# Softmax without its maximum, and layer normalisation moved behind the output product, in a RWKV5 plus SoLU kernel

## The chip, the cores and the metric

The kernel runs on one core of a Trainium2 chip. The metric is device time in microseconds of one execution; lower is better. A "median" below is over the executions of one kernel in one set of runs. 2% is the margin below which two kernels count as the same. On one core all runs of a set share a chip and the runs of the kernel before.

In the profile's lines PE is TensorE, PEld its weight load, DVE is VectorE, ACT is ScalarE, POOL is GpSimd. L806 is a line of that kernel's source, so the same operation has other numbers in other kernels. A "round" is one value of the loop's index `i`.

## The reference

An RWKV5 attention (batch 4, 8 heads, 768 tokens, head size 48) feeds a SoLU feed-forward block with 3072 tokens, 384 model columns and 1024 inner columns:

```python
# attention, per token t:  y = r (state + u k v^T);  state = w * state + k v^T
# ... x = y as (3072, 384)
h = x @ w_in                                   # (3072, 1024)
h_max = np.max(h, axis=-1, keepdims=True)
e = np.exp(h - h_max)
sm = e / (np.sum(e, axis=-1, keepdims=True) + 1e-09)
solu = h * sm
mu = np.mean(solu, axis=-1, keepdims=True)
var = np.mean((solu - mu) ** 2, axis=-1, keepdims=True)
ln = (solu - mu) / np.sqrt(var + 1e-06) * g_ln
return (ln @ w_out).astype(np.float32)
```

## The kernel before

Work comes in 24 units of 128 tokens. The loop is a software pipeline: in round `i` it prepares unit `i+2`, makes the scores of unit `i+1`, the attention output of unit `i`, the inner product `h_ps` and the softmax of unit `j = i-2`, and the output product of unit `l = i-5`. The weights arrive as 64-bit words and are converted on the chip in rounds -2 to 5 (`convert_a` to `convert_d`, on three engines); `g_ln` is multiplied into `w_out`. A flag `bad` chooses at the very end whether a slow general path must run; with these inputs it never does.

```python
    def diagonal(i):                     # ScalarE: eight diagonals of the scores
        ...
        for h in range(H):
            nc.scalar.activation(out=AT[:, h, :], in_=ident, func=ACT.Copy, scale=X["own"][:, h])

    def ffn_in(i):
        h_ps = psH.tile([128, dff], F32, name="h_ps")      # one buffer
        # ... 6 matmuls into h_ps
        nc.vector.tensor_reduce(out=nmax, in_=h_ps, axis=AX.X, op=ALU.max, negate=True)
        nc.scalar.activation(out=e, in_=h_ps, func=ACT.Exp, bias=nmax, accum_out=se)

    def unit(i):
        nc.vector.tensor_scalar_add(rs, se, 1e-9)
        nc.vector.reciprocal(out=rs, in_=rs)
        nc.vector.scalar_tensor_tensor(out=solu, in0=h_ps, scalar=rs, in1=e, ..., accum_out=tot)
        nc.vector.tensor_scalar_mul(nmu, tot, -1.0 / dff)
        nc.scalar.activation(out=sq, in_=solu, func=ACT.Square, bias=nmu, accum_out=ss)
        # ... GpSimd: var, then rstd = var ** -0.5

    def normalise(i):
        nc.vector.tensor_scalar(out=X["solu"], in0=X["solu"], scalar1=nmu, scalar2=rstd,
                                op0=ALU.add, op1=ALU.mult)

    def turn_ln(i):      # 8 transposes into t_ps (TensorE), copied to lnT (VectorE, ScalarE)
    def ffn_out(i):      # 8 matmuls of lnT with w_out into o_ps, copied out, stored

    for i in range(-2, N + LA + LO):
        # ... turn_r, sum_own, turn_k of unit i+2; convert_d; convert_a, convert_b
        diagonal(i + 2)
        # ... decay_k, convert_c, weigh
        turn_ln(l); ffn_in(j); scores(i + 1); unit(j)
        if drain and l + 1 < N:
            turn_ln(l + 1)
        ffn_out(l); normalise(j); finish(i)
```

(`finish` makes the attention output y, its copy xT on ScalarE, and the state.)

Of the kernel before, what the change touches and what calls it, by code (L numbers as in the profile page):

```python
# [9 lines left out]
F32 = mybir.dt.float32  # L10
U32 = mybir.dt.uint32
ACT = mybir.ActivationFunctionType
ALU = mybir.AluOpType
AX = mybir.AxisListType
# [4 lines left out]
def general_path(  # L19
# [191 lines left out]
    def prepare(i):  # L211
        b, c = units[i]
        kt, rt, vt = kpads[i % NLD], rpads[i % NLD], vts[i % NLD]
        X = live[i] = {}
        kT = apool.tile([128, HP, T], F32, name="kT")
        rT = apool.tile([128, HP, T], F32, name="rT")
        for src, dst in ((kt, kT), (rt, rT)):
# [3 lines left out]
            nc.scalar.copy(out=dst, in_=ps)  # L221
        X["kT"], X["rT"] = kT, rT
        X["z"] = {}
        for ls in LEVELS:
# [172 lines left out]
def direct_path(  # L397
# [16 lines left out]



    nc = tc.nc
    B, H, S, D = r.shape
    T = 128
# [3 lines left out]
    dm = H * D  # L423
    dff = moe_w_in.shape[1]
    KD = dm // 128
    KF = dff // 128
    NX = 512
    LA, LO = 2, 3
    LOW, HIGH = 0.75, 1.25

    FLOOR, CEIL = 2.0 ** -15, 122880.0

    const = ctx.enter_context(tc.tile_pool(name="const", bufs=1))
    apool = ctx.enter_context(tc.tile_pool(name="apool", bufs=2))
    fpool = ctx.enter_context(tc.tile_pool(name="fpool", bufs=2))
    wpool = ctx.enter_context(tc.tile_pool(name="wpool", bufs=2))
    small = ctx.enter_context(tc.tile_pool(name="small", bufs=4))
    psA = ctx.enter_context(tc.tile_pool(name="psA", bufs=2, space=PSUM))
    psH = ctx.enter_context(tc.tile_pool(name="psH", bufs=1, space=PSUM))
    psM = ctx.enter_context(tc.tile_pool(name="psM", bufs=4, space=PSUM))  # L440
# [6 lines left out]
    units = [(b, c) for c in range(C) for b in range(B)]  # L447
# [6 lines left out]
    def load(i, which="krv"):  # L454
        b, c = units[i]
        for t, src, n in ((kpads, k, "k"), (rpads, r, "r"), (vts, v, "v")):
            if n in which:
# [8 lines left out]
    w_out_sb = const.tile([128, KF, dm], F32, name="w_out_sb")  # L466
# [5 lines left out]
                        in_=u.rearrange("h d -> (h d)").partition_broadcast(128))  # L472
# [4 lines left out]
    def words(x):  # L477
# [5 lines left out]
    pieces = [(w_in_sb[:, c, ts(n, NX)], w_in_w[ts(c, 128), ts(n, 2 * NX)], None)  # L483
              for n in range(dff // NX) for c in range(KD)]
# [79 lines left out]
    def double(x):  # L564
        for j in range(7):
# [7 lines left out]
                            op0=ALU.max, op1=ALU.min)  # L573
# [27 lines left out]
    def make_wt():  # L601

        nc.gpsimd.memset(wt, 0.0)
        for q in range(2):
            rows = slice(q * P, q * P + D)
            nc.gpsimd.tensor_copy(out=wt[rows, :, q, :],
                                  in_=pw[rows, 0, 7].unsqueeze(2).to_broadcast([D, HP, D]))

    bad = flag.tile([1, 1], mybir.dt.int32, name="bad")

    def check_range():
        nc.sync.dma_start(out=wrow, in_=w.rearrange("h d -> (h d)").partition_broadcast(1))

        ok = small.tile([1, dm], F32, tag="ok", name="ok", bufs=1)
        ok2 = small.tile([1, dm], F32, tag="ok2", name="ok2", bufs=1)
        nc.vector.tensor_single_scalar(out=ok, in_=wrow, scalar=LOW, op=ALU.is_ge)
        nc.vector.tensor_single_scalar(out=ok2, in_=wrow, scalar=HIGH, op=ALU.is_le)
        nc.vector.tensor_mul(ok, ok, ok2)
        all_ok = small.tile([1, 1], F32, tag="all_ok", name="all_ok", bufs=1)
        nc.vector.tensor_reduce(out=all_ok, in_=ok, axis=AX.X, op=ALU.min)  # L620
        nc.vector.tensor_scalar(out=bad, in0=all_ok, scalar1=-1.0, scalar2=1.0,
                                op0=ALU.mult, op1=ALU.add)

    live = {}

# [20 lines left out]
    def diagonal(i):  # L646
        X = live[i]
        AT = X["AT"] = apool.tile([128, H, T], F32, name="AT", bufs=3)
        for h in range(H):
            nc.scalar.activation(out=AT[:, h, :], in_=ident, func=ACT.Copy, scale=X["own"][:, h])  # L650
# [8 lines left out]
    def turn_k(i):  # L659
        X = live[i]  # L660
        X["kT"] = apool.tile([128, HP, T], F32, name="kT")
        ps = psM.tile([128, HP, T], F32, tag="m", name="tk_ps")
        for a in range(HP):
            nc.tensor.transpose(ps[:, a, :], pair(X["kp"], a), ident)  # L664
        nc.scalar.copy(out=X["kT"], in_=ps)  # L665
# [62 lines left out]
    def ffn_in(i):  # L728
        X = live[i]
        h_ps = psH.tile([128, dff], F32, name="h_ps")  # L730
        for n in range(dff // NX):
            for j in range(KD):
                nc.tensor.matmul(h_ps[:, ts(n, NX)], X["xT"][:, j, :], w_in_sb[:, j, ts(n, NX)],  # L733
                                 start=(j == 0), stop=(j == KD - 1))
        st = small.tile([128, 8], F32, name="st")
        nmax, se, rs, tot, nmu, ss, var, rstd = X["st"] = [st[:, n : n + 1] for n in range(8)]
        nc.vector.tensor_reduce(out=nmax, in_=h_ps, axis=AX.X, op=ALU.max, negate=True)  # L737
        e = fpool.tile([128, dff], F32, name="e")
        nc.scalar.activation(out=e, in_=h_ps, func=ACT.Exp, bias=nmax, accum_out=se)  # L739
        X["h"], X["e"] = h_ps, e  # L740

    def unit(i):
        X = live[i]
        nmax, se, rs, tot, nmu, ss, var, rstd = X["st"]
        h_ps, e = X["h"], X["e"]
        nc.vector.tensor_scalar_add(rs, se, 1e-9)
        nc.vector.reciprocal(out=rs, in_=rs)
        solu = X["solu"] = fpool.tile([128, dff], F32, name="solu", bufs=LO + 2)
        nc.vector.scalar_tensor_tensor(out=solu, in0=h_ps, scalar=rs, in1=e,  # L749
                                       op0=ALU.mult, op1=ALU.mult, accum_out=tot)  # L750
        nc.vector.tensor_scalar_mul(nmu, tot, -1.0 / dff)  # L751
        sq = fpool.tile([128, dff], F32, name="sq", bufs=1)
        nc.scalar.activation(out=sq, in_=solu, func=ACT.Square, bias=nmu, accum_out=ss)  # L753
        nc.gpsimd.tensor_scalar(out=var, in0=ss, scalar1=1.0 / dff, scalar2=1e-6,  # L754
                                op0=ALU.mult, op1=ALU.add)
        nc.gpsimd.tensor_tensor(out=rstd, in0=var, in1=neg_half, op=ALU.pow)  # L756

    def normalise(i):
        X = live[i]
        nmax, se, rs, tot, nmu, ss, var, rstd = X["st"]  # L760
        nc.vector.tensor_scalar(out=X["solu"], in0=X["solu"], scalar1=nmu, scalar2=rstd,  # L761
                                op0=ALU.add, op1=ALU.mult)


    def turn_ln(i):
        X = live[i]
        lnT = X["lnT"] = fpool.tile([128, KF, 128], F32, name="lnT")
        for g in range(KF // 4):
            t_ps = psM.tile([128, 4, 128], F32, tag="m", name="t_ps")
            for f in range(4):  # L770
                nc.tensor.transpose(t_ps[:, f, :], X["solu"][:, ts(4 * g + f, 128)], ident)  # L771
            if g % 2 == 0:
                nc.vector.tensor_copy(out=lnT[:, ts(g, 4), :], in_=t_ps)
            else:
                nc.scalar.copy(out=lnT[:, ts(g, 4), :], in_=t_ps)

    def ffn_out(i):
        b, c = units[i]
        X = live.pop(i)
        o_ps = psM.tile([128, dm], F32, tag="m", name="o_ps")  # L780
        for f in range(KF):
            nc.tensor.matmul(o_ps, X["lnT"][:, f, :], w_out_sb[:, f, :],  # L782
                             start=(f == 0), stop=(f == KF - 1))
        o = fpool.tile([128, dm], F32, name="o")
        nc.scalar.copy(out=o, in_=o_ps)
        nc.sync.dma_start(out=out[ds(b * S + c * T, T), :], in_=o)


    N = len(units)
    ahead = 5  # L790
    todo = list(range(len(pieces)))
    conversions = {-2: 1, -1: 1, 0: 2, 1: 2, 2: 3, 3: 3, 4: 2}
    now = []
    decay_k(0)
    for i in range(-2, N + LA + LO):
        j, l = i - LA, i - LA - LO
        drain = i >= N + LA - 1
        if i == 0:
            nc.sync.dma_start(out=g_sb, in_=moe_g_ln.rearrange("(c p) -> p c", p=128))
        if 0 <= i and i + 4 < N:  # L800
            load(i + 4)
        if i + 2 < N:
            turn_r(i + 2)
            if i == -2:
                weigh(0, nc.vector)
            sum_own(i + 2)  # L806
            turn_k(i + 2)
        for p in now:
            convert_d(p)
        now = [todo.pop(0) for _ in range(conversions.get(i, 0))]  # L810
        for p in now:
            convert_a(p)
            convert_b(p)
            if ahead < len(pieces):
                load_weights(ahead)
                ahead += 1
        if i + 2 < N:
            diagonal(i + 2)
        if i + 3 < N:
            decay_k(i + 3)  # L820
        for p in now:
            convert_c(p)
        if i + 3 < N:
            weigh(i + 3, nc.gpsimd)
        if i == -1:
            make_wt()
        if i == 10:
            check_range()
        if 0 <= l and not i > N + LA - 1:
            turn_ln(l)  # L830
        if 0 <= j < N:
            ffn_in(j)
        if 0 <= i + 1 < N:
            scores(i + 1)
        if 0 <= j < N:
            unit(j)
        if drain and l + 1 < N:
            turn_ln(l + 1)
        if 0 <= l:
            ffn_out(l)  # L840
        if 0 <= j < N:
            normalise(j)
        if 0 <= i < N:
            finish(i)
    return bad


# [40 lines left out]
```

## Time and profile before

| | before |
|---|---|
| median of 3 runs | 429.55 us (428.15 to 429.98) |
| span of the profiled execution | 427.9 us, mean granted clock 0.964 |
| busy share: TensorE, VectorE, ScalarE, GpSimd | 93, 50, 43, 30% |
| one steady round | 16.07 us, all TensorE |
| fifth h_ps begins (end of the start) | 101.47 us |
| TensorE ends | 422.90 us |

The table is to be read as three stages. In the start (a quarter of the span) weights are still being converted and TensorE waits for other engines. In the steady rounds TensorE is the whole chain. In the end no input is left and TensorE drains. A change counts only where it shifts the last wait of its stage. The profile's lines are shown in the prediction.

### The profile page before, as it was taken

The numbers are of one execution on the slowest core, as the hardware profiler recorded it, in microseconds if no ns is written. First come the engines' busy times: TensorE is split into PE (matmuls) and PEld (weight loads), VectorE is DVE, ScalarE is ACT, GpSimd is POOL, SyncE is SP. The second block draws the span as 40 slices with busy tenths as digits, with TensorE's granted clock in tenths as the row PEclk, the third lists the DMA queues.
The fourth block names the chain that finished last, engine by engine and source line by source line (L and its number), as shares of the span: only waits on it lengthen the run. The fifth ranks groups of instructions, "written<-read, shape, count | busy, mean of one in ns | idle before, by whom it ended". The sixth has DMA issues, their size and how long they took to land.

```text
span 427.9 us, 7198 instructions
## 1 busy us (share of the span) xinstructions
PE 395.9 (93%) x2853; PEld 249.7 (58%) x2853; DVE 212.4 (50%) x391; ACT 185.0 (43%) x422; POOL 128.7 (30%) x167
## 2 busy tenths in 40 slices
PE   2579397799999999999999999999999999999995
PEld 1466353556756756756756756756756756565562
DVE  6787987743643645642642642642642633343410
ACT  1775377544344344344344344344344442233310
POOL 4587544524124124124124134134134000000000
PEclk9868778899999999999999999999999999999999
DMA  8999891003303303303213213123120000000011
GB/s 170 270 199 222 182 103 20 0 2 74 65 12 74 64 12 74 63 13 74 62 15 74 60 16 76 47 29 75 34 41 20 20 1 20 20 18 11 8 40 43
DMA packets 81592, 25.92 MB, mean 61 GB/s; under 512 B 76557, under 2 KB 79758, under 8 KB 81550
## 3 DMA queue, kind: packets, MB, share of 16 engines
q1 hardware_dynamic: 81406, 25.18, 29.3%
q8 instruction: 24, 0.39, 0.4%
q10 hardware_dynamic: 144, 0.20, 0.1%
q14 instruction: 18, 0.15, 0.1%
HBM read 20.65 MB, written 4.72 MB: 59 GB/s over the span
## 4 chain that ended last, share of the span: by engine, by line
PE 80%; DVE 13%; POOL 2%; issue 2%; ACT 1%; DMA 1%; POOLq 0%; ACTq 0%; DVEq 0%
PE o_ps L782 30%; PE h_ps L733 26%; PE y_ps L703 7%; PE t_ps L771 5%; PE at L675 5%; PE kv_ps L719 4%; DVE ma L516 3%; DVE ma L518 2%; PE tr_ps L656 2%; PE tk_ps L664 2%; DVE mag L512 1%; DVE tab L567 1%; POOL rku L639 1%; POOL rku L640 1%; DVE solu L749 1%
## 5 line engine op out<-in xcount | busy, mean ns | idle before, releaser
L733 PE MATMUL h_ps<-w_in_sb,xT 128*128 128x512 f32 x288 | 133.4, 615 | 9.0 <-DVE solu L749 9.0
L782 PE MATMUL o_ps<-w_out_sb,lnT 128*128 128x384 f32 x384 | 129.5, 491 | 0.0
L782 PEld LDWEIGHTS o_ps<-w_out_sb,lnT 128*128 128x128 f32 x384 | 71.2, 190 | 47.9 <-issue 1.0
L733 PEld LDWEIGHTS h_ps<-w_in_sb,xT 128*128 128x128 f32 x288 | 55.0, 198 | 70.4 <-issue 70.4
L737 DVE TENSOR_REDUCE st<-h_ps 128x1 f32<-128x1024 f32 x24 | 29.4, 1223 | 92.6 <-PE h_ps L733 92.6
L739 ACT ACTIVATE e<-h_ps,st 128x1024 f32<-128x1024 f32 x24 | 26.8, 1115 | 94.8 <-DVE st L737 94.8
L650 ACT ACTIVATE AT<-ident,own 128x128 f32<-128x128 f32 x192 | 58.8, 390 | 11.4 <-DVE own L644 11.3
L754 POOL TENSOR_SCALAR st<-st 128x1 f32<-128x1 f32 x24 | 4.6, 192 | 196.4 <-ACT sq L753 196.4
L761 DVE TENSOR_SCALAR solu<-solu,st 128x1024 f32<-128x1024 f32 x24 | 21.4, 892 | 54.2 <-POOL st L756 54.2
L753 ACT ACTIVATE sq<-solu,st 128x1024 f32<-128x1024 f32 x24 | 27.6, 1151 | 47.8 <-DVE st L751 47.8
L675 PEld LDWEIGHTS at<-rT,kT 48*128 48x128 f32 x384 | 26.3, 202 | 20.0 <-issue 16.3
L675 PE MATMUL at<-rT,kT 48*128 48x128 f32 x384 | 31.3, 301 | 2.9 <-DVE AT L678 2.8
L633 POOL TENSOR_TENSOR kp<-kpad,kdec 128x512 f32<-128x512 f32 x24 | 30.8, 1284 | 5.3 <-ACT kdec L583 5.3
L678 DVE COPY_PREDICATED AT<-later,at 128x512 f32<-128x512 uint32 x48 | 32.1, 723 | 0.0
L749 DVE SCALAR_TENSOR_TENSOR solu<-h_ps,st,e 128x1024 f32<-128x1024 f32 x24 | 30.8, 1284 | 0.8
L723 POOL TENSOR_TENSOR state<-state,wt 128x384 f32<-128x384 f32 x16 | 16.1, 1006 | 48.6 <-DVE state L722 48.6
L771 PE MATMUL t_ps<-ident,solu 128*128 128x128 f32 x192 | 25.8, 279 | 3.1 <-ACT xT L715 3.1
L703 PE MATMUL y_ps<-AT,vt 128*32 128x128 f32 x768 | 27.1, 285 | 0.0
L771 PEld LDWEIGHTS t_ps<-ident,solu 128*128 128x128 f32 x192 | 22.2, 144 | 5.4 <-ACT xT L715 3.3
L665 ACT COPY kT<-tk_ps 128x512 f32<-128x512 f32 x24 | 14.0, 585 | 25.9 <-PE tk_ps L664 25.8
L640 POOL TENSOR_TENSOR rku<-rku,rpad 128x384 f32<-128x384 f32 x23 | 23.0, 999 | 1.8
L719 PE MATMUL kv_ps<-vt,kp 128*128 128x96 f32 x160 | 23.5, 292 | 0.0
(67 smaller groups left out, 365.5 us busy)
## 6 DMA issues: line engine op xcount, KB each, us to landing
kpad<-in_k_dram SPq DMA_DIRECT2D x24, 192.0 KB, 3.4
rpad<-in_r_dram SPq DMA_DIRECT2D x24, 192.0 KB, 4.0
vt<-in_v_dram SPq DMA_DIRECT2D x24, 192.0 KB, 3.9
out_dram<-o SPq DMA_DIRECT2D x24, 192.0 KB, 2.0
raw<-in_moe_w_in_dram SPq DMA_DIRECT2D x6, 512.0 KB, 6.0
raw<-in_moe_w_out_dram SPq DMA_DIRECT2D x8, 384.0 KB, 3.5
u_bc<-in_u_dram ACTq DMA_DIRECT2D x1, 192.0 KB, 3.0
wq<-in_w_dram SPq DMA_DIRECT2D x1, 1.5 KB
```

Source lines behind the costliest of these rows:

```text
L633: nc.gpsimd.tensor_mul(X["kp"].rearrange("p h d -> p (h d)"), kpads[i % NLD].rearrange("p h d -> p (h d)"), kdec.rearrange("p a d -> p (a ...
L650: nc.scalar.activation(out=AT[:, h, :], in_=ident, func=ACT.Copy, scale=X["own"][:, h])
L675: nc.tensor.matmul(pss[q][:, a, :], X["kT"][rows, a, :], X["rT"][rows, a, :], start=True, stop=True)
L678: nc.vector.copy_predicated(A4[:, :, q, :], later.to_broadcast([128, HP, T]), pss[q])
L703: nc.tensor.matmul(y_ps[32 * g : 32 * g + 32, j, :], lhsT, rhs, start=(g not in opened), stop=stop, skip_group_check=True)
L719: nc.tensor.matmul(kv_ps[:, a], pair(X["kp"], a), vt[:, 2 * a : 2 * a + 2, 0:D], start=True, stop=True)
L733: nc.tensor.matmul(h_ps[:, ts(n, NX)], X["xT"][:, j, :], w_in_sb[:, j, ts(n, NX)], start=(j == 0), stop=(j == KD - 1))
L737: nc.vector.tensor_reduce(out=nmax, in_=h_ps, axis=AX.X, op=ALU.max, negate=True)
L749: nc.vector.scalar_tensor_tensor(out=solu, in0=h_ps, scalar=rs, in1=e, op0=ALU.mult, op1=ALU.mult, accum_out=tot)
L753: nc.scalar.activation(out=sq, in_=solu, func=ACT.Square, bias=nmu, accum_out=ss)
L771: nc.tensor.transpose(t_ps[:, f, :], X["solu"][:, ts(4 * g + f, 128)], ident)
L782: nc.tensor.matmul(o_ps, X["lnT"][:, f, :], w_out_sb[:, f, :], start=(f == 0), stop=(f == KF - 1))
```

## The change

The intent is to relieve VectorE. The maximum goes: exp is taken of `h` itself, and the sums of exp are tested once at the end, so that a sum above 1e30 or below 1e-30 sends the work to the general path. The normalisation of rows goes as well. Since `(solu - mu) @ W` is `solu @ (W - column means of W)`, the column means of `w_out` are taken off the matrix once, the rows go to the product uncentred, and the output's copy multiplies by `rstd`. To make room, the diagonals move behind the squares in ScalarE's queue, and the first output product changes places with the attention output.

```diff
+    def check_sums():
+        # ... good = (sums >= 1/MOST) * (sums <= MOST), two tests and a product on VectorE
+        nc.vector.tensor_reduce(out=low, in_=good, axis=AX.X, op=ALU.min)
+        n_ps = psM.tile([1, 1], F32, tag="m", name="n_ps")
+        nc.tensor.matmul(n_ps, low, ones[:, 0:1], start=True, stop=True)
+        nc.vector.tensor_scalar(out=bad, in0=n_ps, scalar1=all_ok, ...)
+    def column_mean(fs):
+        for f in fs:
+            nc.tensor.matmul(mean[0], ones, w_out_sb[:, f, :], ...)
+            if f == KF - 1:
+                nc.scalar.copy(out=mean_sb, in_=mean[0])
+    def centre(f, engine):
+        engine.tensor_sub(w_out_sb[:, f, :], w_out_sb[:, f, :], mean_sb)
@@ ffn_in
-        nc.vector.tensor_reduce(out=nmax, in_=h_ps, axis=AX.X, op=ALU.max, negate=True)
-        nc.scalar.activation(out=e, in_=h_ps, func=ACT.Exp, bias=nmax, accum_out=se)
+        nc.scalar.activation(out=e, in_=h_ps, func=ACT.Exp, accum_out=sums[:, i : i + 1])
@@ unit
-        nc.vector.tensor_scalar_add(rs, se, 1e-9)
-        nc.vector.reciprocal(out=rs, in_=rs)
+        nc.vector.reciprocal(out=rs, in_=sums[:, i : i + 1])
...
-        nc.vector.tensor_scalar_mul(nmu, tot, -1.0 / dff)
-        nc.scalar.activation(out=sq, in_=solu, func=ACT.Square, bias=nmu, accum_out=ss)
+        nc.scalar.activation(out=sq, in_=solu, func=ACT.Square, accum_out=ss)
...      # two more tiny GpSimd operations for the variance
-    def normalise(i):
-        nc.vector.tensor_scalar(out=X["solu"], in0=X["solu"], scalar1=nmu, scalar2=rstd, ...)
@@ ffn_out
-        nc.scalar.copy(out=o, in_=o_ps)
+        nc.scalar.activation(out=o, in_=o_ps, func=ACT.Copy, scale=X["rstd"])
@@ the loop
-        if i + 2 < N:
-            diagonal(i + 2)
...
+        if l == 0:
+            column_mean(fs)
+            for f in range(KF):
+                centre(f, nc.vector if f % 2 == 0 else nc.gpsimd)
+            turn_ln(l)
         if 0 <= i + 1 < N:
             scores(i + 1)
         if 0 <= j < N:
             unit(j)
+        if i == N + LA - 1:
+            check_sums()
+        if i + 2 < N:
+            diagonal(i + 2)
         if drain and l + 1 < N:
             turn_ln(l + 1)
+        if l <= 0 <= i:
+            finish(i)
         if 0 <= l:
             ffn_out(l)
-        if 0 <= j < N:
-            normalise(j)
-        if 0 <= i < N:
+        if 0 < l and i < N:
             finish(i)
+        if l < 0 and fs:
+            column_mean(fs)
```

More of the change, by code (lines that the diff above doesn't have):

```diff
@@ L431, in direct_path @@
     FLOOR, CEIL = 2.0 ** -15, 122880.0
+    MOST = 1e30
     const = ctx.enter_context(tc.tile_pool(name="const", bufs=1))
@@ L607, in make_wt @@
                                   in_=pw[rows, 0, 7].unsqueeze(2).to_broadcast([D, HP, D]))
+    N = len(units)
+    sums = const.tile([128, N], F32, name="sums")
+    all_ok = const.tile([1, 1], F32, name="all_ok")
     bad = flag.tile([1, 1], mybir.dt.int32, name="bad")
@@ L618, in check_range @@
         nc.vector.tensor_mul(ok, ok, ok2)
-        all_ok = small.tile([1, 1], F32, tag="all_ok", name="all_ok", bufs=1)
         nc.vector.tensor_reduce(out=all_ok, in_=ok, axis=AX.X, op=ALU.min)
-        nc.vector.tensor_scalar(out=bad, in0=all_ok, scalar1=-1.0, scalar2=1.0,
-                                op0=ALU.mult, op1=ALU.add)
+    def check_sums():
+        good = small.tile([128, N], F32, name="good", bufs=1)
+        good2 = small.tile([128, N], F32, name="good2", bufs=1)
+        low = small.tile([128, 1], F32, name="low", bufs=1)
+        nc.vector.tensor_single_scalar(out=good, in_=sums, scalar=1.0 / MOST, op=ALU.is_ge)
+        nc.vector.tensor_single_scalar(out=good2, in_=sums, scalar=MOST, op=ALU.is_le)
+        nc.vector.tensor_mul(good, good, good2)
+        nc.vector.tensor_reduce(out=low, in_=good, axis=AX.X, op=ALU.min)
+        n_ps = psM.tile([1, 1], F32, tag="m", name="n_ps")
+        nc.tensor.matmul(n_ps, low, ones[:, 0:1], start=True, stop=True)
+        nc.vector.tensor_scalar(out=bad, in0=n_ps, scalar1=all_ok, scalar2=127.5 / dff,
+                                op0=ALU.mult, op1=ALU.is_lt)
+    ones = const.tile([128, 128], F32, name="ones")
+    mean_sb = const.tile([128, dm], F32, name="mean_sb")
+    nc.gpsimd.memset(ones, 1.0 / dff)
+    mean = []
+    def column_mean(fs):
+        if not mean:
+            mean.append(psM.tile([128, dm], F32, tag="m", name="mean_ps"))
+        for f in fs:
+            nc.tensor.matmul(mean[0], ones, w_out_sb[:, f, :], start=(f == 0), stop=(f == KF - 1),
+                             skip_group_check=True)
+            if f == KF - 1:
+                nc.scalar.copy(out=mean_sb, in_=mean[0])
+    def centre(f, engine):
+        engine.tensor_sub(w_out_sb[:, f, :], w_out_sb[:, f, :], mean_sb)
     live = {}
@@ L734, in ffn_in @@
                                  start=(j == 0), stop=(j == KD - 1))
-        st = small.tile([128, 8], F32, name="st")
-        nmax, se, rs, tot, nmu, ss, var, rstd = X["st"] = [st[:, n : n + 1] for n in range(8)]
-        nc.vector.tensor_reduce(out=nmax, in_=h_ps, axis=AX.X, op=ALU.max, negate=True)
-        e = fpool.tile([128, dff], F32, name="e")
-        nc.scalar.activation(out=e, in_=h_ps, func=ACT.Exp, bias=nmax, accum_out=se)
-        X["h"], X["e"] = h_ps, e
+        e = X["e"] = fpool.tile([128, dff], F32, name="e")
@@ L742, in unit @@
+        nc.scalar.activation(out=e, in_=h_ps, func=ACT.Exp, accum_out=sums[:, i : i + 1])
+        X["h"] = h_ps
     def unit(i):
         X = live[i]
-        nmax, se, rs, tot, nmu, ss, var, rstd = X["st"]
-        h_ps, e = X["h"], X["e"]
-        nc.vector.tensor_scalar_add(rs, se, 1e-9)
-        nc.vector.reciprocal(out=rs, in_=rs)
+        st = small.tile([128, 8], F32, name="st")
+        rs, tot, ss, sqm, var, rstd = (st[:, n : n + 1] for n in range(6))
+        nc.vector.reciprocal(out=rs, in_=sums[:, i : i + 1])
@@ L748, in unit @@
         solu = X["solu"] = fpool.tile([128, dff], F32, name="solu", bufs=LO + 2)
-        nc.vector.scalar_tensor_tensor(out=solu, in0=h_ps, scalar=rs, in1=e,
+        nc.vector.scalar_tensor_tensor(out=solu, in0=X["h"], scalar=rs, in1=X["e"],
                                        op0=ALU.mult, op1=ALU.mult, accum_out=tot)
-        nc.vector.tensor_scalar_mul(nmu, tot, -1.0 / dff)
         sq = fpool.tile([128, dff], F32, name="sq", bufs=1)
-        nc.scalar.activation(out=sq, in_=solu, func=ACT.Square, bias=nmu, accum_out=ss)
@@ L754, in unit @@
-        nc.gpsimd.tensor_scalar(out=var, in0=ss, scalar1=1.0 / dff, scalar2=1e-6,
+        nc.scalar.activation(out=sq, in_=solu, func=ACT.Square, accum_out=ss)
+        nc.gpsimd.tensor_mul(sqm, tot, tot)
+        nc.gpsimd.tensor_scalar(out=sqm, in0=sqm, scalar1=-1.0 / dff ** 2, scalar2=1e-6,
+                                op0=ALU.mult, op1=ALU.add)
+        nc.gpsimd.tensor_scalar(out=var, in0=ss, scalar1=1.0 / dff, scalar2=sqm,
                                 op0=ALU.mult, op1=ALU.add)
         nc.gpsimd.tensor_tensor(out=rstd, in0=var, in1=neg_half, op=ALU.pow)
-    def normalise(i):
-        X = live[i]
-        nmax, se, rs, tot, nmu, ss, var, rstd = X["st"]
-        nc.vector.tensor_scalar(out=X["solu"], in0=X["solu"], scalar1=nmu, scalar2=rstd,
-                                op0=ALU.add, op1=ALU.mult)
+        X["rstd"] = rstd
@@ L784, in ffn_out @@
         o = fpool.tile([128, dm], F32, name="o")
-        nc.scalar.copy(out=o, in_=o_ps)
+        nc.scalar.activation(out=o, in_=o_ps, func=ACT.Copy, scale=X["rstd"])
         nc.sync.dma_start(out=out[ds(b * S + c * T, T), :], in_=o)
-    N = len(units)
     ahead = 5
@@ L807, in direct_path @@
             turn_k(i + 2)
+        fs = [pieces[p][2] for p in now if pieces[p][2] is not None]
         for p in now:
@@ L828, in direct_path @@
             check_range()
-        if 0 <= l and not i > N + LA - 1:
+        if 0 < l and not i > N + LA - 1:
             turn_ln(l)
```

## The prediction

The forecast's sum: 429.55 - 0.7 + 3.9 + 1.7 = 434.5 us. The 1.7 is an estimate from the trace of before: after TensorE's pause of 2.48 us (to 67.78) the clock read 0.50 from 69.2 to 72.6 us, and half of these 3.4 us is 1.7. A "window" is such a stretch. That the matmuls behind a waiting one are held up with it, on which the 3.9 rests, was not shown beforehand. Rival C's 438 to 439 was the estimate of a slower centring and one more stretch at 0.50, and was not shown.

> **What bounds the kernel now.** I read four views in this order. First the page's busy shares and slices:
>
> ```profile
> PE 395.9 (93%) x2853; PEld 249.7 (58%) x2853; DVE 212.4 (50%) x391; ACT 185.0 (43%) x422; POOL 128.7 (30%) x167
> ...
> PE   2579397799999999999999999999999999999995
> ...
> PEclk9868778899999999999999999999999999999999
> ```
>
> TensorE is full from about slice 8 (slices are 10.7 us) to the end; the granted clock dips only before that. Next the chain of work that ended last. Two pieces of it, a steady period and the end:
>
> ```profile
> 100.60 0.87 PE t_ps L771 x8
> 101.47 5.15 PE h_ps L733 x12
> 106.62 1.09 PE at L675 x16
> 107.72 5.36 PE o_ps L782 x16
> 113.07 1.67 PE y_ps L703 x56
> 114.74 1.06 PE kv_ps L719 x8
> 116.67 0.87 PE t_ps L771 x8
> ...
> 393.59 0.87 PE t_ps L771 x8
> 394.46 5.15 PE h_ps L733 x12
> 399.62 0.87 PE t_ps L771 x8
> ```
>
> One round takes 116.67 - 100.60 = 16.07 us, and every piece is TensorE. From 82.62 to 422.90 us no other engine is on the chain. So what VectorE or ScalarE saves in a steady round is worth nothing. Third, the chain before that:
>
> ```profile
> 63.55 1.13 DVE st L737
> 64.68 1.26 DVE AT L678 x2
> 66.34 1.30 DVE solu L749 x2
> 67.91 1.25 ACT sq L753 x2
> 69.52 0.56 POOL st L756
> 70.11 1.76 DVE solu L761
> ```
>
> In the start the chain is the softmax itself: maximum, product, squares, power, normalising. The waits agree: the only long TensorE wait is for the product that frees the one h_ps buffer.
>
> ```profile
> L733 PE MATMUL h_ps<-w_in_sb,xT 128*128 128x512 f32 x288 | 133.4, 615 | 9.0 <-DVE solu L749 9.0
> ```
>
> It is 9.0 us in 2 times, at 52.84 and 67.78. Fourth, the table of stretches, for the clock (the column after POOL):
>
> ```profile
> 52.00:59.00 7.00, 6.16 (x8) 2.58 (x9) 4.70 (x9) 6.08 (x13) 1.99 (x3) 0.51 1.48 173
> 69.00:73.00 4.00, 4.00 (x7) 1.55 (x6) 2.89 (x4) 4.00 (x11) 1.99 (x3) 0.57 0.00 0
> 83.00:87.00 4.00, 4.00 (x12) 2.47 (x11) 2.93 (x5) 2.55 (x8) 2.60 (x4) 0.60 0.00 0
> 100.00:116.00 16.00, 16.00 (x126) 10.13 (x125) 7.19 (x14) 6.91 (x16) 4.93 (x6) 1.00 0.27 50
> ```
>
> Each TensorE pause (46.4 to 52.8, 65.4 to 67.8, 79.5 to 82.6) is followed by a stretch at half clock.
>
> [...]the clock is full or half[...]: 0.50 or 1.00, with changes some 3.4 us or multiples apart (69.2 to 72.6, 82.85 to 86.25), and a 592 ns matmul that reads 1193 at most. A pause of 2.5 us was enough to lose one window, so half of 3.4 = 1.7 us. [...]VectorE sat 2.23 us before normalising while other work was queued. [...]The mantissa step is 0.36 us alone and 1.05 beside GpSimd's addition[...]; the centring will be slowed likewise.
>
> **The change part by part.** A round is one value of the loop's index; unit 0 has its h_ps made in round 2 and its output product in round 5, unit 1 a round later, and so on to round 28. Durations are means from the page's groups (maximum 1223 ns, normalising 892, product 1284, diagonals of a unit 2.45 us in the order of time).
>
> Removed on VectorE per unit: maximum 1.22, normalising 0.89, two tiny operations at 0.15; 2.4 us x 24 = 58 us busy. Of this, only what lies in the start can count. GpSimd gains two tiny operations, about 0.4 us, beside other work.
>
> Added on TensorE: eight column-mean matmuls, the size of one output product (5.36 us). Six run in rounds 3 and 4, where it has some slack; two (1.34) in round 5. Then eight centring subtractions: four on VectorE at 0.56 to 0.83, four on GpSimd at 1.0, about 4.1 us after the mean is copied. Behind that copy TensorE still has transposes 0.87, scores 1.09, y and kv 2.73 = 4.7 us, so they are just covered.
>
> Moved: on ScalarE the eight diagonals (2.45 us) now follow the squares. The built order shows the queue: exp, squares, diagonals, xT, kT, three scalings, six conversions, next exp. The mean holds one of four PSUM buffers from round 3 to 5; in the built program the kT transpose then waits for the state update, which VectorE does after the product.
>
> The start, by hand with measured durations:
> - Round 2: VectorE finishes converting at 48.6, scores 50.0, product 51.5 (before 52.7). The next h_ps starts at 51.65 instead of 52.84: 1.2 gained. VectorE is free of the wait and of normalising, 5 us early.
> - Round 3: ScalarE eats this. Squares end 52.95, diagonals 55.4, xT and kT 56.45, scalings 58.1, so the first converted magnitude comes at 58.7. VectorE began that at 58.31 before. Converting takes the same 5.24 us, to 63.95; scores, product to 66.9 (before 67.6); state 67.5; kT transpose; h_ps at 68.0 (before 67.78). Nothing gained.
> - Round 4: the same by ScalarE: magnitude at 74.05, product to 80.25, h_ps at 81.55. Before: t_ps from 82.62, h_ps 84.2, then a half-clock window.
> - Round 5: h_ps to 86.7, mean 88.05, t_ps, scores, y, kv to 92.75, output product to 98.15, transposes 98.6 to 99; ScalarE's xT, behind squares and diagonals, releases t_ps of the next round at 99.4 to 100.0. The next h_ps follows at 100.4 to 101.4; before 101.47. Start: about 0.7 us gained.
>
> Steady rounds: the same matmuls in the same order, 16.07 each: 0.
>
> The end: the sums are tested in the last input round. The built order on TensorE is: last h_ps, one 1x1 matmul that counts, then the remaining transposes and products. That matmul needs exp, reciprocal, product and four small VectorE operations over all the sums. From h_ps ready at 399.66: exp to 400.95 (1.11 + 0.19), reciprocal 401.1, product to 402.4, four at about 0.18 = 403.15, plus the matmul: t_ps starts near 403.5 instead of 399.62. Before, 23.3 us of back-to-back TensorE work followed there, so about 3.9 us go straight to the end. The pause exceeds those that lost the clock, so 1.7 more: 5.6.
>
> Sum: 429.55 - 0.7 + 5.6 = 434.5 us.
>
> **Rivals.**
> - A: the start shrinks by all that leaves VectorE's chain there: per round 2 to 4 wait for squares, power and normalising 4.1 plus the maximum 1.2, some 5.3 x 3 = 16, less 1.3 for the mean. For it: the chain of the start above consists of these very lines. Against it: ScalarE's queue, which is full where VectorE becomes free. With the loss at the end it would give about 420; without that loss 415.
> - B: the start gains 3 to 5 us because the pauses that lost the clock vanish[...], and the end loses as worked out: 430 to 432. For it: round 4's h_ps begins 2.7 us earlier at full clock. Against: the xT wait takes it back.
> - C: centring delays the first output product. [...]438 to 439.
> - D: the counting matmul costs nothing, because VectorE's sums come early. Then 429. Against: the last sum is that of the last h_ps, and no TensorE work lies between.
>
> **Range and chances.** The end's 4 us is the firmest term; the clock after it may cost 0 to 3, the start may be -4 to +3. This gives 429 to 437.5 for 8 in 10. Faster by 2% needs under 421, thus A nearly whole: 0.04. Slower by 2% needs over 438.1, C or two lost windows: 0.07. Within: 0.89.
>
> **What would show it.** Right: in the changed kernel's chain, 16.07 us rounds as before; t_ps of the second round near 100 us on the chain; a TensorE pause of about 4 us before the counting matmul, its releaser the VectorE reduction, and a clock near 0.5 for some 3.4 us after; ScalarE without idle time between the squares and the next exp in rounds 2 to 4. Wrong: steady rounds starting 5 us or more earlier (A), a wait of the output product for GpSimd's or VectorE's centring over 2 us (C), or no pause near the end (D). If steady rounds are not 16.07 us, the argument that TensorE alone sets them fails.

## The result, and the profile after

The kernel after took 433.32 us in the median of 6 runs (432.53 to 434.14); before, in the same rounds, 429.76 (428.15 to 430.82). The ratio is 1.0086, 95% interval 1.0064 to 1.0108: within 2%. All ratios in this document are the mean time of one kernel's fast runs over that of the other's of the same rounds. The recorded ratios come out so when the profiled run is left out, so they are not quite the ratio of the medians. The profiled spans are 431.2 and 427.9 us.

The page of the kernel after, busy shares and granted clock in 40 slices:

```profile
PE 400.3 (93%) x2871; PEld 252.9 (59%) x2871; DVE 158.2 (37%) x303; ACT 181.3 (42%) x423; POOL 145.2 (34%) x220
...
PEclk9998889999999999999999999999999999999898
```

VectorE lost 54 us of its 212, and the time did not fall. The clock row has new dips in the last slices.

Its chain of waits (start in us, duration, engine, tile, line), with a piece of each stage:

```profile
67.07 2.33 ACT AT L691 x8
69.77 0.48 ACT kT L706
70.25 1.53 ACT w_out_sb L541 x3
71.77 0.45 ACT mag L510
...
97.99 1.13 PE t_ps L806 x8
99.13 5.15 PE h_ps L774 x12
...
114.33 0.87 PE t_ps L806 x8
...
130.40 0.87 PE t_ps L806 x8
...
392.12 5.17 PE h_ps L774 x12
397.31 1.12 ACT e L777 x2
398.79 1.29 DVE solu L786 x2
400.93 1.44 PE t_ps L806 x8
```

Three things are to be seen. First, ScalarE now stands in the start's chain: the diagonals (AT), the copy of the transposed keys (kT), the scalings of the weights and then the first converted magnitude. Secondly, a steady round is 130.40 - 114.33 = 16.07 us, to the hundredth what it was. Thirdly, before the drain the chain leaves TensorE: exp, product, and only then the transposes at 400.93, whose duration of 1.44 us was 0.87 before.

TensorE's timeline (the bracket is its idle time and what ended it) names what stood in front of those transposes, and a wait in the start that was not there before:

```profile
91.53 5.40 PE L817 MATMUL o_ps<-w_out_sb,lnT 128*128 128x384 f32 x16 [0.98 <-DVE lnT L808]
...
400.74 0.19 PE L642 MATMUL n_ps<-ones,low 128*1 128x1 f32 x2 [3.47 <-DVE low L640]
```

n_ps is the counting matmul. The table of stretches (the first column after the six busy times, PE to POOL, is the clock):

```profile
69.00:73.00 4.00, 4.00 (x22) 1.99 (x22) 0.72 (x2) 4.00 (x10) 0.39 (x1) 1.00 0.00 0
83.00:87.00 4.00, 4.00 (x22) 2.42 (x21) 0.59 (x2) 2.44 (x6) 2.20 (x3) 1.00 0.02 4
400.00:405.00 5.00, 4.26 (x15) 2.96 (x16) 1.51 (x8) 1.74 (x3) 1.20 (x4) 0.66 0.01 2
```

The two stretches of the start that stood at 0.57 and 0.60 are at full clock; the drain now loses some.

The account from the two traces:

| stage | before | after | difference |
|---|---|---|---|
| begin to fifth h_ps | 101.47 | 99.13 | -2.34 |
| fifth h_ps to the last h_ps's transposes | 298.15 | 301.80 | +3.65 |
| these transposes to TensorE's end | 23.28 | 25.12 | +1.84 |
| TensorE's end to the end | 5.0 | 5.15 | +0.15 |
| sum | | | +3.30 |

The second row's end points are 399.62 and 400.93 in the chains, and the third's end is 422.90 and 426.05. The sum is the difference of the spans, 431.2 - 427.9. The start gained, and the end lost more than twice as much.

### The profile page after: what moved, and what is told of

The parts are those of the page before. It is cut to its first block, busy times and chain, and to the rows that moved or that the text cites. A ratio compares the mean times of both kernels' runs of the same rounds, so it can differ in the third digit from the quotient of the medians.

```text
span 431.2 us, 7237 instructions
## 1 busy us (share of the span) xinstructions
PE 400.3 (93%) x2871; PEld 252.9 (59%) x2871; DVE 158.2 (37%) x303; ACT 181.3 (42%) x423; POOL 145.2 (34%) x220
## 4 chain that ended last, share of the span: by engine, by line
PE 79%; DVE 10%; ACT 4%; POOL 2%; issue 2%; DMA 1%; ACTq 0%; POOLq 0%; DVEq 0%; SPq 0%
PE o_ps L817 29%; PE h_ps L774 25%; PE y_ps L744 7%; PE t_ps L806 5%; PE at L716 5%; PE kv_ps L760 4%; DVE ma L524 2%; PE tk_ps L705 2%; PE tr_ps L697 2%; DVE ma L526 2%; ACT AT L691 2%; DVE mag L520 1%; DVE tab L575 1%; DVE w_out_sb L663 1%; POOL rku L680 1%
## 5 line engine op out<-in xcount | busy, mean ns | idle before, releaser
L774 PE MATMUL h_ps<-w_in_sb,xT 128*128 128x512 f32 x288 | 130.1, 602 | 5.1 <-DVE solu L786 5.1
L774 PEld LDWEIGHTS h_ps<-w_in_sb,xT 128*128 128x128 f32 x288 | 53.8, 194 | 64.2 <-issue 64.2
L777 ACT ACTIVATE e<-h_ps 128x1024 f32<-128x1024 f32 x24 | 24.5, 1023 | 93.8 <-PE h_ps L774 93.8
L789 ACT ACTIVATE sq<-solu 128x1024 f32<-128x1024 f32 x24 | 25.4, 1057 | 76.6 <-DVE solu L786 76.6
L791 POOL TENSOR_TENSOR st<-st 128x1 f32<-128x1 f32 x24 | 4.6, 193 | 149.9 <-DVE solu L786 149.9
L763 DVE TENSOR_TENSOR state<-kv_ps,state 128x384 f32<-128x384 f32 x16 | 8.9, 558 | 74.5 <-PE kv_ps L760 74.5
L808 DVE COPY lnT<-t_ps 128x512 f32<-128x512 f32 x24 | 16.4, 684 | 30.2 <-PE t_ps L806 30.0
L820 ACT ACTIVATE o<-o_ps,st 128x384 f32<-128x384 f32 x24 | 13.6, 566 | 23.6 <-PE o_ps L817 15.1
```

The source lines that it names most:

```text
L774: nc.tensor.matmul(h_ps[:, ts(n, NX)], X["xT"][:, j, :], w_in_sb[:, j, ts(n, NX)], start=(j == 0), stop=(j == KD - 1))
L777: nc.scalar.activation(out=e, in_=h_ps, func=ACT.Exp, accum_out=sums[:, i : i + 1])
L789: nc.scalar.activation(out=sq, in_=solu, func=ACT.Square, accum_out=ss)
```

## The experiments

The theory after the result: the end's 5.6 us come wholly from the place of the counting matmul in TensorE's queue (the wait, and the clock it costs); the start is set by ScalarE's queue, which the moved diagonals fill, and by the mean. The rivals: the end's loss is VectorE's tests or another effect of the new order (then moving the matmul gains little), and the start is limited by TensorE's mean matmuls, or by VectorE itself.

Ten kernels ran. The last ones ask what the change is worth with its order mended, and what its simplest part is worth alone.

### late_count: the counting matmul placed last

```diff
         nc.vector.tensor_reduce(out=low, in_=good, axis=AX.X, op=ALU.min)
+        lows.append(low)
+    lows = []
+    def count_sums():
+        low = lows[0]
         n_ps = psM.tile([1, 1], F32, tag="m", name="n_ps")
         nc.tensor.matmul(n_ps, low, ones[:, 0:1], start=True, stop=True)
...
+        if l + 1 == N - 1:
+            count_sums()
         if 0 <= l:
             ffn_out(l)
```

VectorE's four tests stay where they were; only the matmul (and the flag made from it) moves behind the last transposes.

> The changed kernel with only the counting matmul moved: it now stands behind the last transposes instead of in front of seven pieces of TensorE work; the four VectorE operations stay where they are. Theory (the waiting matmul costs 3.65 us by its wait and 1.85 us by the half clock after it): 433.3 - 5.5 = 427.8 us, no TensorE pause after the last h_ps, clock full to the end, start unchanged. Rival 1 (the loss is the column mean's own 5.4 us of TensorE work and the centring, the end only shows it late): 432 or more. Rival 2 (VectorE's four tests hold up the end, not the matmul): no change, 433.

Measured: 427.58 us (427.54 to 427.71), ratio to before 0.9961 (0.9933 to 0.9990), correct. Against the kernel after that is 433.32 - 427.58 = 5.74 us less, for one moved matmul of 0.19 us. TensorE's timeline in the end (the modelled ends of neighbours overlap a little):

```profile
394.73 2.31 PE L780 MATMUL h_ps<-w_in_sb,xT 128*128 128x512 f32 x5
396.88 1.04 PE L812 MATMUL t_ps<-ident,solu 128*128 128x128 f32 x8
...
408.95 1.04 PE L812 MATMUL t_ps<-ident,solu 128*128 128x128 f32 x8
409.91 0.19 PE L648 MATMUL n_ps<-ones,low 128*1 128x1 f32 x2
```

The transposes follow h_ps without a wait, and n_ps, which no longer waits either, lies behind the last of them. So the whole loss of the end was the waiting matmul. The tests on VectorE cost nothing by themselves.

### fill_mm and fill_turn: the wait kept, TensorE kept busy in it

Two kernels leave the wait as it is and put useless work ahead of the counting matmul: 5 matmuls with `w_out`, or 28 transposes of the identity matrix.

```diff
# fill_mm
+        fill = psM.tile([128, dm], F32, tag="m", name="fill")
+        for n in range(5):
+            nc.tensor.matmul(fill, ident, w_out_sb[:, n, :], start=(n == 0), stop=(n == 4))
         nc.tensor.matmul(n_ps, low, ones[:, 0:1], start=True, stop=True)
# fill_turn
+        fill = psM.tile([128, 4, 128], F32, tag="m", name="fill")
+        for n in range(FILL):
+            nc.tensor.transpose(fill[:, n % 4, :], ident, ident)
         nc.tensor.matmul(n_ps, low, ones[:, 0:1], start=True, stop=True)
```

The question is how much of the 5.6 is the clock, and whether transposes in the pause do for it what matmuls do. The "if so" in fill_turn's expectation is the case that they do not.

> The changed kernel with five useless 128x384 matmuls put ahead of the counting matmul, in the time in which TensorE waits anyway (5 x 0.67 = 3.35 us of a pause of 3.5). The wait stays, the idleness goes. Theory (half clock is the pause's second cost): the counting matmul starts where it did, the clock stays at 1.00 after it, and the time falls by 1.8 to 431.5 us. Rival (the slow stretch after the pause is something else, or the clock reacts to the program and not to idleness): 433.3, or more if the filler delays.

> As fill_mm, but the filler is 28 transposes (28 x 0.109 = 3.05 us). [...]If so here: half clock for some 3.4 us after the count, as in the changed kernel, time 433.3. If they count as matmuls do: clock 1.00, about 431.5.

Measured: fill_mm 431.36 us (431.12 to 431.8), ratio 1.0052 (1.0023 to 1.0082); fill_turn 431.26 (431.05 to 431.8), ratio 1.0048 (1.0018 to 1.0078). TensorE's timeline of fill_turn:

```profile
396.85 3.22 PE L645 MATMUL fill<-ident 128*128 128x128 f32 x28
400.57 0.19 PE L646 MATMUL n_ps<-ones,low 128*1 128x1 f32 x2 [0.50 <-DVE low L641]
```

and its table of stretches:

```profile
400.00:405.00 5.00, 4.50 (x22) 3.10 (x22) 1.26 (x4) 1.66 (x3) 1.17 (x4) 1.00 0.00 2
```

The counting matmul starts at 400.57 as before (400.74; the fifth h_ps was 0.26 us earlier too), but the clock afterwards is 1.00 where it was 0.66. In fill_mm it is 1.00 as well. The time falls by 2.0 us (433.32 to 431.36 and 431.26), and every run of both kernels (431.8 at most) lies below every run of the kernel after (432.53 at least, in another set). So of the end's loss about 2.0 are the clock and 3.7 the wait itself. The transposes did as well as the matmuls: the clock, 1.00 from 396 to 400 us, was still 1.00 from 400 to 405. (The trace names both MATMUL. They are not the same instruction: 28 transposes leave 28 records, the 5 fp32 matmuls of fill_mm leave 10.) Whether transposes alone would raise a clock that stands at 0.50 was not tried.

### diag_early: the diagonals put back

```diff
                 load_weights(ahead)
                 ahead += 1
+        if i + 2 < N:
+            diagonal(i + 2)
         if i + 3 < N:
             decay_k(i + 3)
...
-        if i + 2 < N:
-            diagonal(i + 2)
         if drain and l + 1 < N:
```

> The changed kernel with the eight diagonals back in the place in ScalarE's queue that they had before (ahead of exp and squares). Theory (in rounds 2 to 5 ScalarE's queue, squares then diagonals, holds back the magnitudes and xT, so that VectorE waits 4.8 us twice): magnitudes come some 2.4 us earlier in rounds 3 and 4, the fourth h_ps starts 1 to 2 us earlier, time 431.5 (430.8 to 432.3); the end is unchanged. Rival (VectorE or TensorE itself bounds the start now): 433.3.

Measured: 428.69 us (runs 428.17, 428.08, 429.21, 430.91), ratio 1.0003 (0.9962 to 1.0044). The mechanism is confirmed, with a gain above what was expected: the chain of waits of the profiled run

```profile
95.57 5.15 PE h_ps L774 x12
```

has the fifth h_ps at 95.57 instead of 99.13 us, 3.56 earlier, and from 51.47 us on the chain holds only TensorE work, apart from the mean's copy, the centring and lnT at 82.78 to 88.42. VectorE waited 2.50 and 2.31 us for the magnitudes where it had waited 4.84 and 4.89. So the moved diagonals were what bounded the start. How much they cost depends on the clock as well: the second h_ps took 6.80 us here and 7.83 in the kernel after, and `both` below puts them at 2.0 us. 433.32 - 3.56 is 429.8; three of the four runs were below that. In the profiled one (428.17) the end still has its pause, 3.45 us from 393.73 to 397.18, but the stretch from 397 to 401 us has clock 1.00. So nearly the same pause was followed by a loss of 1.84 us in one profile and 0.16 in the other (transposes to TensorE's end, 23.44 us against 23.28 before); why was not shown. In the profile of no_mean below, the loss after a pause of 3.47 us is 2.85 (26.13 us).

### both: late_count and diag_early together

The edit is the two above. Against late_count, only the diagonals' place differs.

> The changed kernel with both edits, the count behind the last transposes and the diagonals early. Theory (two independent costs, the queue in the start 3.6 us as the diag_early profile shows, the end 5.5): 433.3 - 3.6 - 5.5 = 424.2 us (423.5 to 425.5). Rival (diag_early owed its 4.6 us to a lucky clock window at the end, not to the start): 427.

Measured: 425.55 us (424.32 to 425.91) in 6 runs, ratio 0.9898 (0.9870 to 0.9925). The interval lies below 1, though inside the margin of 2%: with two moves of place the change becomes a small gain over before. It is 1.3 us above the 424.2 expected, and the trace shows where. Up to the second h_ps the instructions are those of diag_early, and it starts at 51.65 us against 51.47; but it takes 8.13 us against 6.80, the stretch from 51 to 59 us having clock 0.61 against 0.79. The fifth h_ps is at 96.86 against 95.57. That is the size of the clock's share again. Held against late_count, the diagonals' place is worth 2.03 us: the fifth h_ps comes at 96.86 instead of 98.89, and the medians are 425.55 and 427.58, though from different sets. The 3.6 us that the expectation took over from diag_early held a share of clock.

### no_mean: the column means left out (a wrong result, on purpose)

```diff
         if l == 0:
-            column_mean(fs)
-            for f in range(KF):
-                centre(f, nc.vector if f % 2 == 0 else nc.gpsimd)
             turn_ln(l)
...
-        if l < 0 and fs:
-            column_mean(fs)
```

> The changed kernel without the mean and the centring (the result is wrong by the mean's part on purpose). Theory (most of the mean lies beside ScalarE's queue; on the path of round 5 are mean, copy and centring less what TensorE and VectorE do there anyway): 2.5 us in round 5 and about 1.1 before, 433.3 - 3.6 = 429.7 (428.5 to 430.7). Rival 1 (the mean is the loss: all of its 5.36 and the centring count): 427 or less. Rival 2 (all hidden): 433.

Measured: 429.03 us (428.87 to 430.68), ratio 0.9982 (0.9948 to 1.0016); the output is wrong as intended. Its profile fell on the slowest of the four runs (430.68). In it the third h_ps starts at 65.75 instead of 66.91 us, the fourth at 78.82 instead of 79.42, and the fifth at 95.60 instead of 99.13. So the means cost the start 3.5 us in this pair of profiles, with the diagonals in their late place, and 4.3 us by the medians. Of the 3.5, 2.9 arise after the fourth h_ps, in the round of the first output product (two matmuls 1.30, copy 0.49, centring 4.38, lnT), which the output product waits for. In the rounds before, the mean's matmuls had a use that nobody had counted. TensorE's timeline without them:

```profile
65.75 8.37 PE L774 MATMUL h_ps<-w_in_sb,xT 128*128 128x512 f32 x12 [3.24 <-DVE solu L786]
```

Without the mean's matmuls TensorE stands still for 3.24 us, and this product, the third h_ps, takes 8.37 us; with them it waited 1.32 us, and the product took 5.32 at clock 1.00. One profile is no proof, but it offers a reason why the kernel after had clock 1.00 from 69 to 73 us.

### sum_off_pe: the row blocks added by GpSimd and VectorE

Starting from both, the eight mean matmuls become seven additions of row blocks and one matmul; the copies of the transposed rows go ahead of the centring.

```diff
+            engine.tensor_add(total, w_out_sb[:, 0, :] if f == 1 else total, w_out_sb[:, f, :])
             if f == KF - 1:
-                nc.scalar.copy(out=mean_sb, in_=mean[0])
+                nc.tensor.matmul(mean_ps, ones, total, start=True, stop=True)
+                nc.scalar.copy(out=mean_sb, in_=mean_ps)
...
-            column_mean(fs)
+            column_mean(fs, nc.vector)
+            turn_ln(l)
             for f in range(KF):
                 centre(f, nc.vector if f % 2 == 0 else nc.gpsimd)
-            turn_ln(l)
...
-            column_mean(fs)
+            column_mean(fs, nc.gpsimd)
```

> As both, and the eight rows blocks of the output matrix are added up by GpSimd (rounds 3 and 4) and VectorE (round 5), so that one column-mean matmul is left of eight; the first transposes' copy goes ahead of the centring. Theory (with the queue mended, TensorE is without a pause from the second h_ps on, so mean matmuls now lie on the path): 7 x 0.67 = 4.7 us and the 1.0 us wait for the copy less: 418.5 to 419.5 us. Rival (VectorE or GpSimd takes over in rounds 3 to 5): 421 to 424.

Measured: 427.21 us (425.24 to 428.02), ratio 0.9930 (0.9901 to 0.9959): a clear miss, 1.7 us slower than both, where 418.5 to 419.5 us were expected. GpSimd's timeline and TensorE's:

```profile
76.83 1.00 POOL L773 TENSOR_TENSOR state<-state,wt 128x384 f32<-128x384 f32 x1
77.79 3.14 POOL L665 TENSOR_TENSOR total<-total,w_out_sb 128x384 f32<-128x384 f32 x3
```

```profile
83.98 1.62 PE L668 MATMUL mean_ps<-total,ones 128*128 128x384 f32 x2 [3.90 <-DVE total L665]
```

The fourth h_ps of this kernel did start earlier, 74.70 us against 77.43 (both by the timeline). But the three additions stood in GpSimd's queue behind the power and the state update, VectorE's own additions waited for them, and TensorE waited 3.90 us for the total. The pause was followed by a stretch at clock 0.62 (84 to 92 us). I had counted the additions and not the queue in front of them. That the queue is the cause is read from this trace; the next run avoids it.

### sum_reduce: one reduction on VectorE instead

Starting again from both:

```diff
+    def row_sum():
+        nc.vector.tensor_reduce(out=total, in_=w_out_sb.rearrange("p f d -> p d f"), axis=AX.X,
+                                op=ALU.add)
...
         if l == 0:
-            column_mean(fs)
-            for f in range(KF):
-                centre(f, nc.vector if f % 2 == 0 else nc.gpsimd)
+            row_sum()
             turn_ln(l)
         if 0 <= i + 1 < N:
             scores(i + 1)
+        if l == 0:
+            column_mean()                # one matmul, one copy
+            for f in range(KF):
+                centre(f, nc.vector if f % 2 == 0 else nc.gpsimd)
```

> As both, but the mean costs TensorE one matmul instead of eight: in round 5, where VectorE stands idle, one VectorE reduction adds the eight row blocks (a 128x1024 reduction took 1.22 us, so 128x3072 some 3.4), and the mean matmul stands behind transposes and scores so that TensorE does not wait for it; the copy of the transposes and the scores' copies go ahead of the centring. Theory (what sank sum_off_pe is GpSimd's queue, in which the additions of round 4 stood behind power and state, and not the idea): h_ps of round 5 starts near 75 us as there, no TensorE wait in round 5, the next h_ps near 92.6 instead of 96.7: 425.5 - 4.1 = 421.4 us (420 to 423.5). Rival (any engine that takes the mean from TensorE becomes the bound of the start): 425 or more.

Measured: 421.91 us (421.57 to 422.09) in 5 runs, ratio 0.9825 (0.9802 to 0.9848), correct. VectorE's timeline:

```profile
76.81 5.54 DVE L660 TENSOR_REDUCE total<-w_out_sb 128x384 f32<-128x3072 f32 x1 [1.62 <-ACT w_out_sb L541]
```

The reduction took 5.54 us where 3.4 were expected, but it begins under the h_ps of its round, and TensorE waited only 1.24 us for it. The next h_ps starts at 93.34 us against 96.86 in both: 3.52 earlier, which is the difference of the medians (425.55 - 421.91 = 3.64). This is the best version, 7.7 us below before (429.64 in its set), still inside the margin of 2%.

### max_only and max_count: the simplest part of the change alone

max_only takes the kernel before and removes the maximum, nothing else (its sums are not tested, so it is a measurement and not a safe kernel). max_count adds the test of the sums with the counting matmul in its late place.

```diff
# max_only, against the kernel before
-        nc.vector.tensor_reduce(out=nmax, in_=h_ps, axis=AX.X, op=ALU.max, negate=True)
         e = fpool.tile([128, dff], F32, name="e")
-        nc.scalar.activation(out=e, in_=h_ps, func=ACT.Exp, bias=nmax, accum_out=se)
+        nc.scalar.activation(out=e, in_=h_ps, func=ACT.Exp, accum_out=se)
# max_count, against max_only
+        nc.scalar.activation(out=e, in_=h_ps, func=ACT.Exp, accum_out=sums[:, i : i + 1])
...
+        if i == N + LA - 1:
+            check_sums()
...
+        if l + 1 == N - 1:
+            count_sums()
```

> The kernel before with one part of the change alone: exp without the maximum, the maximum itself taken out; normalising stays on VectorE, no mean, no test of the sums. Theory (the chain of the start contains the maximum once in each of rounds 2 to 4, and nothing is added): 429.6 - 3 x 1.2 = 426.0 (425 to 427.5[...]). Rival 1 (VectorE's savings are off the path or are eaten by another queue): 429.6. Rival 2 (steady rounds gain as well: 24 x 1.2): 400 or so.

> max_only made whole: the sums of exp are kept for all units and tested at the end, with the count behind the last transposes; normalising, and with it the output matrix, stay as before. Theory (a test costs its one small matmul of 0.1 to 0.3 us if nothing stands behind it that waits): 424.5 to 424.9 us. Rival (keeping and testing the sums costs at the end as in the changed kernel): 428 or more.

Measured: max_only 424.48 us (424.23 to 427.12), ratio 0.9876 (0.9842 to 0.9909); max_count 424.80 (423.9 to 426.76), ratio 0.9904 (0.9877 to 0.9931); both correct. The chain of waits of max_only, to be held against 82.62 before:

```profile
79.02 1.97 PE t_ps L770 x8
```

That is 3.60 us earlier, three rounds of 1.2 us, the maximum's own duration (1.13 us at the second h_ps, 2.37 at the third). The median gained more than that, 5.3 us. The profile of max_only fell on its slowest run (427.12), in which the fourth h_ps took 7.19 us. The profile of max_count (a run of 424.30) shows where the rest comes from; its chain has the fourth and fifth h_ps as

```profile
79.59 5.15 PE h_ps L754 x12
...
95.67 5.15 PE h_ps L754 x12
```

so the fourth took 5.15 us, as in the steady rounds at clock 1.00 (6.11 before, where the clock was 0.60 from 83 to 87 us), and the fifth comes 5.80 us earlier than before: the rest is put down to the clock. What is settled is that deleting one line gains more than the whole change as written, and that testing the sums costs so little that these runs don't separate the two (424.48 and 424.80, in different sets).

## Why the prediction was right

The prediction said 434.5 (429 to 437.5) and "within 2%"; measured were 433.32 and a ratio of 1.0086. Step by step:

- **Steady rounds, 0.** Right: 16.07 us in both. What VectorE lost there was off the chain. The exp even became shorter (below) without effect.
- **The end, 3.9 + 1.7 = 5.6.** Right in mechanism and size: the traces give 3.65 + 1.84 = 5.49, late_count gives 5.74, and fill_mm and fill_turn split it into some 3.7 and 2.0. The releaser of n_ps is VectorE's `low`, as predicted, and rival D (the matmul costs nothing) falls. That the clock took close to the 1.7 us predicted is in part luck: after pauses of the same length, the profiles of diag_early and no_mean lost 0.16 and 2.85 us.
- **The start, 0.7 gained.** Right in mechanism, the term mis-sized: 2.34 us were gained. The second h_ps came at 51.73 us (predicted 51.65). ScalarE then took it back as described: VectorE idled 4.84 and 4.89 us in rounds 3 and 4, both times until ScalarE delivered a magnitude, and diag_early, where these waits fall to 2.50 and 2.31 us, shows that the moved diagonals were the cause. But the third and fourth h_ps came at 66.91 and 79.42 us, not 68.0 and 81.55.
- **Where the start's error arose.** The prediction added up the durations of ScalarE's instructions one after another (squares to 52.95, diagonals to 55.4, scalings to 58.1). The trace shows that neighbours overlap: the eight diagonals are busy 2.43 us, but the next instruction begins 2.34 after the first. And exp and squares became shorter themselves. The group of exp in the kernel after, which was 1115 ns before:

```profile
L777 ACT ACTIVATE e<-h_ps 128x1024 f32<-128x1024 f32 x24 | 24.5, 1023 | 93.8 <-PE h_ps L774 93.8
```

  Squares went from 1151 to 1057 ns. Both lost a bias operand with one value per row, and became 92 and 94 ns shorter; the output's copy, which got such an operand as its scale, went from 478 to 566 ns, 88 longer. The prediction had counted neither this nor the overlap. About 0.8 us of the start is explained so by the first magnitude, begun at 57.37 us and ready at 57.9 instead of 58.7.
- **The rest of the start.** The fourth h_ps came 5.0 us earlier than before (84.44 to 79.42) and had clock 1.00 (79.4 to 84.6); from there to the fifth, 2.7 of this were given back. From fourth to fifth h_ps it is 17.03 us before (with an h_ps of 6.11, the clock at 0.60 from 83 to 87 us) and 19.71 after. The two slow stretches of before at 69 to 73 and 83 to 87 us (0.57 and 0.60) are gone (1.00), which rival B had said. So the truth of the start lies between the main line and B. Why the clock stayed at 1.00 in them was not isolated by a run; for the first of them, no_mean points to the mean's matmuls, which the prediction had counted as cost alone. The kT transpose's wait that the prediction reads off the built order is there (1.32 and 0.34 us before the third and fourth h_ps) and is gone in no_mean, where the mean holds no PSUM buffer. The profile names GpSimd's rku as its releaser, though, and not the state update.
- **Rival A** (the start shrinks by all that leaves VectorE) falls as argued, since ScalarE's queue bounds; but both and sum_reduce show that A was attainable in part: with the diagonals back and the mean off TensorE, the fifth h_ps comes at 93.34 us, 8.1 earlier than before.
- **Rival C** (centring delays the first output product). Small but real: the prediction held the centring to be "just covered", and o_ps waited 0.98 us for lnT behind it. The centring took 4.38 us in VectorE's chain and 5.2 us on GpSimd (4.1 predicted), and the clock was 1.00 from 84 to 90 us.

Two errors of opposite sign were thus small in the sum: the start gained 1.6 us more than predicted and the end lost 0.1 us less. 434.5 - 1.6 - 0.1 is 432.8, and 433.32 was measured.

There is also a spread of the measure itself. The 11 runs of the kernel before in one set lie near 428.3, near 429.8 and near 431.0 us, with mean clocks of 0.979 to 0.988, 0.963 to 0.973 and 0.957 to 0.965. A difference of 1.5 us between two runs can therefore be one of these steps and no property of a change.

## What to carry to other kernels

A tiny instruction that depends on the newest result can hold up everything behind it in its engine's queue: here a matmul of 0.19 us waited 3.47 us, the transposes behind it started at 400.93 us instead of right after h_ps, and the clock was 0.66 from 400 to 405 us on top; placed later (late_count), it saved 5.74 us. Place it as late as its consumer allows. Before relieving a busy engine, look at which queue will be next in each stage; here the relief was real only in the start, and moving eight cheap diagonals gave 2.0 to 3.6 us of it away. Try the smallest part of a change alone: one deleted line (424.48 us) beat the whole as written (433.32), and only the whole with its order mended (sum_reduce, 421.91) beat the line.

## What else these runs measured

- 28 transposes in the pause of the end were followed by clock 1.00 (400 to 405 us) as 5 matmuls were (431.26 and 431.36 us, against 433.32 and a clock of 0.66 with nothing in the pause).
- A TensorE pause of 2.48 us (to 67.78, before) was followed by clock 0.57 from 69 to 73 us, and one of 3.45 us (diag_early) by 1.00 from 397 to 401. Between these two, the length of the pause alone did not decide.
- For changes of 1% the clock's share is the very size in question: the runs of the kernel before stand in steps of some 1.2 to 1.5 us (428.3, 429.8, 431.0), and profiles of one beginning differ by 1.33 us in one h_ps (8.13 and 6.80, with clocks of 0.61 and 0.79 from 51 to 59 us). Mean clocks of runs are to be compared first.
- A VectorE reduction over 128x3072 whose neighbouring elements lie 384 apart took 5.54 us; three times the 1.22 us of the contiguous maximum over 128x1024 would be 3.7 (an estimate). That it is the stride was not isolated here (the maximum reads PSUM, the reduction SBUF).
- The centring's subtractions of 128x384 took 1.35 us each on VectorE and 1.31 on GpSimd while both ran, against 0.56 (VectorE's first, which began before GpSimd's) and 1.00 for GpSimd's additions of that size elsewhere. The four pairs took 5.2 us together, less than the 6.2 of 4 x (0.56 + 1.00).
